# Own zeros, an identity without DMA, bias rows spread by GpSimd, and gate and value weights decoded as one block

## The chip, the cores and the metric

The kernel runs on one core of a Trainium2 chip. The metric is the device time of one execution in microseconds (us), the lower the better; the median of several runs is given. The engines are TensorE (PE, with its weight loads as PEld), VectorE (DVE), ScalarE (ACT), GpSimd (POOL) and SyncE (SP, which here only issues DMAs). Each engine takes its instructions strictly in the order in which they stand in its own program. DMAs are issued from the queues of SP, ACT and POOL and share 16 DMA engines.

## What is computed

Eight batches of eight heads, 576 positions, 64 dimensions a head, then a gated feed-forward layer over the 4608 tokens:

```python
scores = (1 / sqrt(D)) * q @ k.T                  # per batch and head, causal
cum = cumsum(maximum(s, 0.0), axis=-1)
bias = -(cum[:, :, :, None] - cum[:, :, None, :])
scores = where(causal, -1e9, scores + minimum(bias, 0.0))
attn = softmax(scores)                            # 1e-9 added to the sum
x = (attn @ v) with heads side by side            # 4608 x 512
gate = 1 / (1 + exp(-(x @ w_gate)))               # 512 x 1536
out = (gate * (x @ w_val)) @ w_out                # 1536 x 512
```

q, k, v and s are float32. The three weight matrices are float64, and the kernel reads them as pairs of 32-bit words.

## The kernel before

**The order of the work.** One loop of ticks (L673) runs through the 64 heads, five ticks a head, one for each tile of query rows (64, then four of 128). In a tick the code emits the scores of one tile, then for earlier tiles the mask, the row maximum, the exponential, and the product with v. Feed-forward units are placed between the ticks: a unit is one group of 256 tokens by one of 12 blocks of 128 hidden columns. The code runs through this program in its own order, and a scheduler then fixes the order of each engine's instructions and of the DMAs, before the run, by planned times; attention steps of the first heads carry a higher priority (`first()`), so weight work goes into gaps that the plan has. Nothing is reordered at run time.

**The start.** `ident` (L83 to L92) is the identity matrix with which PE transposes q, k, the exponentials and x. It is made by counting along a row (L88), writing the count to DRAM and reading it back as a column, `place` (L90, L91), and comparing the two (L92). `junk` (L95 to L97) is a buffer whose result nobody reads, and which takes one `affine_select` on POOL. The cumulative sums of the bias are made for all heads at once: s is loaded (L131), clipped (L133), and scanned against `zero` (L134 to L137); the result goes to a DRAM scratch, `cum_d` (L138). Tiles with one tag share its buffers: `junk`, `sp_sb`, `zero` and each head's `cr` have the tag "cr" with two buffers, so the third waits for the first.

**Bias rows.** For each head `load_crow` (L379) reads its row of `cum_d` and writes it to all 128 partitions with one DMA. `bias_row` (L416) subtracts the middle value of the row and multiplies, on DVE, into `rl`. `mask_part` (L424) then lets POOL write the causal limit into the columns of the tile on the diagonal, and the row maximum follows on DVE (L535 for the first eight heads, L437 for the others), which adds the bias row to the scores in PSUM.

**Two kinds of heads.** The first eight heads (`NN`) run in float32: q and k are transposed by PE (L509), scores are float32 matmuls (L526), the exponentials are transposed by PE (L546). The others use pairs of float16 parts and transposing DMAs (L371, L448, L480).

**Weights.** A step of `weight_step` loads one block of a matrix (128 partitions x 512 values, 512 KB as float64) from ACT's queue, turns float64 into float32 with one ACT and three DVE instructions (L233 to L236), sums squares on ACT (L242 or L263), adds them over the partitions on POOL (L246 or L265), forms a power-of-two scale with small DVE instructions (L117 to L127), and splits the block into float16 high (ACT, L256 or L270) and low part (DVE, L257 or L271). Gate and value blocks are separate steps; each has its own scale. The 24 steps of gate and value come first, then 12 of the output matrix. Six staging buffers serve the first 24 steps (two of their own and four in the space of the output weights), two the last 12. From tick `NE` = 44 the loop at L767 emits the units of the first two token groups, with the weight steps three blocks ahead; `hidden_scale` (L273) needs all value and output scales, and the output matmuls (L637) of those groups come after it.

## Time and profile before

| | |
|---|---|
| median of 3 runs | 1249.86 us (1247.86 to 1251.01) |
| the profiled execution | 1257.82 us, of which the span from first to last instruction is 1256.1 |
| granted TensorE clock, mean | 0.967 |
| busy share of the span: PE, DVE, ACT, POOL | 90%, 63%, 61%, 18% |
| DMA | 176.24 MB, mean 140 GB/s, 473412 packets |

The page cuts the span into 40 equal slices of 31.4 us; a digit is the busy share of a slice in tenths:

```profile
PE   1689778989998899989999999999999989999997
DVE  5998878775677757764665566766677667422221
ACT  4898866665666666764656466666676666332221
POOL 1343322221112121210111022212121211000000
PEclk9789889999999999999999999999999999999999
DMA  8764998995988789984665668878888966310000
```

PE is the busiest engine over the whole, but the slices differ: in the first ones DVE and ACT are as full as PE or fuller, and in the first slice PE has hardly begun. A group row of the profile reads: line, engine, operation, output<-input, shapes, how often | busy us in all, mean ns of one | idle time of the engine just before, and what ended most of it. A timeline row reads: start us, duration us, engine, line, operation; in brackets the idle time before it and what ended it.

### The profile page before, as it was taken

How to read it: one execution, taken by the hardware profiler on the slowest of the kernel's cores; microseconds unless marked ns; L12 is line 12 of the kernel's file. 1: busy time of each engine (PE TensorE's matmuls, PEld its weight loads, DVE VectorE, ACT ScalarE, POOL GpSimd, SP SyncE). 2: the span in 40 equal slices, each digit the busy share in tenths (PEclk: the TensorE clock that was granted, in tenths of full speed). 3: DMA queues.
4: the chain of work that ended last, by engine and by line, in shares of the span. 5: the costliest groups of instructions: out<-in, count | busy, mean ns of one | idle time of the engine just before them, and what ended most of it. 6: DMA issues, size and time to landing. Idle time of an engine off the chain costs nothing.

```text
span 1256.1 us, 30839 instructions
## 1 busy us (share of the span) xinstructions
PE 1127.7 (90%) x11924; PEld 875.9 (70%) x11924; DVE 789.6 (63%) x2291; ACT 761.5 (61%) x1553; POOL 227.3 (18%) x541
## 2 busy tenths in 40 slices
PE   1689778989998899989999999999999989999997
PEld 0467566666776787768777776767777777787775
DVE  5998878775677757764665566766677667422221
ACT  4898866665666666764656466666676666332221
POOL 1343322221112121210111022212121211000000
PEclk9789889999999999999999999999999999999999
DMA  8764998995988789984665668878888966310000
GB/s 255 238 179 142 181 188 156 182 181 128 162 164 166 160 161 171 177 163 101 115 146 110 129 143 166 164 154 174 160 163 172 170 118 134 56 29 2 18 18 17
DMA packets 473412, 176.24 MB, mean 140 GB/s; under 512 B 439601, under 2 KB 459058, under 8 KB 473266
## 3 DMA queue, kind: packets, MB, share of 16 engines
q1 hardware_dynamic: 453426, 136.53, 58.1%
q10 hardware_dynamic: 14400, 18.88, 4.9%
q0 software_dynamic: 5440, 18.88, 4.9%
q8 instruction: 93, 1.52, 0.5%
q14 instruction: 53, 0.43, 0.1%
HBM read 75.65 MB, written 9.59 MB: 68 GB/s over the span
## 4 chain that ended last, share of the span: by engine, by line
PE 28%; DMA 23%; issue 23%; ACT 11%; DVE 10%; POOL 2%; SPq 2%; POOLq 0%; ACTq 0%; DVEq 0%
PE gv L607 16%; DMA T<-qk 12%; PE o L637 7%; DMA qk<-in_q_dram 6%; DVE e L437 3%; ACT jq L339 2%; DMA T<-T 1%; DMA vsq<-in_v_dram 1%; PE s L412 1%; PE s L413 1%; ACT e L440 1%; ACT th L612 1%; DVE t L614 1%; ACT qk L366 1%; ACT vsq L151 1%
## 5 line engine op out<-in xcount | busy, mean ns | idle before, releaser
L607 PE MATMUL gv<-x,w 128*128 128x256 f16 (+3 forms) x6912 | 629.1, 249 | 17.1 <-DVE t L614 9.3
L607 PEld LDWEIGHTS <-w 128*128 128x128 f16 x6912 | 543.1, 99 | 78.1 <-issue 19.2
L637 PE MATMUL o<-w2all,h 128*128 128x512 f16 x1296 | 314.2, 379 | 3.2 <-ACT h L622 1.9
L427 POOL TENSOR_SCALAR_AFFINE_SELECT rl<-rl 128x128 f32<-128x128 f32 (+1 forms) x320 | 144.2, 451 | 496.2 <-DVE em L437 248.8
L637 PEld LDWEIGHTS <-h 128*128 128x128 f16 x1296 | 123.3, 98 | 110.9 <-ACT h L622 2.1
L440 ACT ACTIVATE e<-e,em 128x576 f32<-128x576 f32 x280 | 155.1, 556 | 72.6 <-DVE em L437 69.9
L614 DVE SCALAR_TENSOR_TENSOR t<-th,gv 128x256 f32<-128x256 f32 x192 | 80.1, 418 | 167.1 <-ACT th L612 166.7
L612 ACT ACTIVATE th<-gv,scb 128x256 f32<-128x256 f32 (+3 forms) x288 | 110.2, 408 | 117.2 <-PE gv L607 117.1
L437 DVE CUSTOM_DVE_ANT_0 e<-s,rl,qkcf 128x288 f32<-128x288 f32 x280 | 134.5, 484 | 25.4 <-PE s L412 9.7
L622 ACT ACTIVATE h<-t,hsc 128x256 f16<-128x256 f32 x192 | 96.9, 505 | 88.0 <-DVE t L614 87.8
L445 DVE SCALAR_TENSOR_TENSOR p<-e,p 128x1152 f16<-128x1152 f32 x112 | 129.9, 1159 | 31.9 <-ACT p L444 31.0
L623 DVE SCALAR_TENSOR_TENSOR h<-t,hsc,h 128x256 f16<-128x256 f32 x192 | 93.6, 488 | 42.2 <-ACT h L622 40.1
L412 PE MATMUL s<-T 128*128 128x288 f16 x336 | 88.3, 280 | 34.8 <-DVE em L437 29.6
L444 ACT ACTIVATE p<-e 128x1152 f16<-128x1152 f32 x112 | 111.8, 998 | 6.2 <-DMA pt<-p 4.0
L367 DVE SCALAR_TENSOR_TENSOR qk<-qk,qksc,qk 96x384 f16<-96x384 f32 x56 | 34.3, 613 | 104.5 <-ACT qk L366 104.4
L366 ACT ACTIVATE qk<-qk,qksc 96x384 f16<-96x384 f32 x56 | 34.4, 614 | 107.7 <-DMA T<-qk 107.5
L413 PE MATMUL s<-T 128*128 128x288 f16 x336 | 87.9, 283 | 10.8 <-DMA T<-T 10.8
L460 PE MATMUL av<-v,pt 128*128 128x65 f16 x840 | 85.7, 193 | 5.9 <-DMA pt<-p 5.8
L460 PEld LDWEIGHTS <-pt 128*128 128x128 f16 x840 | 77.5, 98 | 12.4 <-DMA pt<-p 7.0
L461 PE MATMUL av<-v,pt 128*128 128x64 f16 x840 | 85.6, 192 | 0.0
L462 PE MATMUL av<-v,pt 128*128 128x65 f16 x840 | 85.3, 194 | 0.0
L461 PEld LDWEIGHTS <-pt 128*128 128x128 f16 x840 | 77.4, 97 | 5.1
(187 smaller groups left out, 1215.3 us busy)
## 6 DMA issues: line engine op xcount, KB each, us to landing
cr<-cum_d SPq DMA_DIRECT2D x64, 288.0 KB, 4.3
vsq<-in_v_dram POOLq DMA_DIRECT2D x32, 288.0 KB, 4.3
out_dram<-osb POOLq DMA_DIRECT2D x36, 256.0 KB, 3.9
v<-in_v_dram SPq DMA_DIRECT2D x64, 128.0 KB, 3.7
qk<-in_q_dram SPq DMA_DIRECT2D x28, 288.0 KB, 3.8
qk<-in_k_dram SPq DMA_DIRECT2D x28, 288.0 KB, 4.8
T<-T SPq DMA_DIRECT2D x112, 72.0 KB, 2.6
ws<-in_moe_w_out_dram ACTq DMA_DIRECT2D x12, 512.0 KB, 4.0
```

The source lines that it names most:

```text
L412: nc.tensor.matmul(ps[:, : b_ - a], lhs, T[i][:, 0, a:b_], start=True, stop=False)
L413: nc.tensor.matmul(ps[:, : b_ - a], lhs, T[i][:, 2, a:b_], start=False, stop=True)
L427: nc.gpsimd.affine_select(rl[i][:, q0:w], rl[i][:, q0:w], pattern=[[-1, m]], compare_op=ALU.is_ge, fill=-MASKED if i < NN else MASKED, bas ...
L437: nc.vector.tensor_tensor_reduce(e_t[t][:, a:b_], ps[:, : b_ - a], rl[i][:, a:b_], c, init, ALU.add, ALU.min, acc)
L440: nc.scalar.activation(e_t[t][:, :w], e_t[t][:, :w], AF.Exp, bias=init, scale=-1.0)
L444: nc.scalar.activation(p_s[h_][:, 0], e_s[h_], AF.Copy, scale=PSCALE)
L445: nc.vector.scalar_tensor_tensor(p_s[h_][:, 1], e_s[h_], PSCALE, p_s[h_][:, 0], ALU.mult, ALU.subtract)
L460: nc.tensor.matmul(AV[i][:, t], hi, v_[:, D : 2 * D + 1], start=kb == 0, stop=False)
L461: nc.tensor.matmul(AV[i][:, t, 0:D], hi, v_[:, 0:D], start=False, stop=False)
L607: nc.tensor.matmul(ps[:, gv, a:e], w1[f][:, cc, gv, wl], x_of(b, cc)[:, xl, c0 + a : c0 + e], start=(c == 0), stop=(c == 3 * NC - 1))
L612: nc.scalar.activation(th[:, a:e], ps[:, 0, a:e], AF.Tanh, scale=scb[b][:, f : f + 1])
L637: nc.tensor.matmul(ps[:m], h[:, hl, tt * P : tt * P + m], w2[f][:, wl], start=(f == 0 and c == 0), stop=(f == NF - 1 and c == 2))
```

## The change

Six things are changed together.

1. `ident` is made on DVE alone: a count of 32 columns, transposed in blocks of 32 x 32 (`nc.vector.transpose`), and four comparisons of 32 x 32. `count` and `junk` lie in a buffer of the tag "x16"; the two DMAs and `place` are gone. The load of s is moved up to this place.
2. `zero` lies in a buffer of the tag "T", set before `sp_sb`.
3. The middle value is subtracted once for all heads (`rel`), and `rel` is what goes to DRAM.
4. `load_crow` reads one partition's row (for head 0 it takes the row in SBUF) and POOL spreads it with `partition_broadcast`. In the first eight heads that tile is the bias row; for the others `bias_row` only multiplies.
5. Gate and value block of one f are one step of 1024 columns, with one decode, one sum of squares, one scale and one split. There are 12 such steps and 12 of the output matrix; three staging buffers of twice the size serve the first 12, halves of one of them the last 12. `invw` and the new `wfield` have two rows in place of three, and the inverses of the scales are formed for three blocks at once (for the output matrix, twelve).
6. The pace of the steps changes: two at the first tick and six by tick 32; from tick 44 on, three at a time at every third f. As the list has 24 steps in place of 36, the bound `f + NF + WLA` (L775) now lets in all 12 output steps at unit 12; before it let in three there and one more at each unit after.

```diff
@@ -81,28 +81,30 @@
     for t, (q0, m, w) in enumerate(TILES):
         nc.gpsimd.memset(e_t[t][:, w:], 0.0)
     ident = cp.tile([P, P], F32, name="ident")
-    count = wp.tile([P, S], F32, tag="rl", name="count")[:, :P]
-    place = cp.tile([P, 1], F32, name="place")
-    nc.vector.memset(ident, 0.0)
-    nc.vector.memset(count, 1.0)
-    nc.vector.tensor_tensor_scan(count, count, ident, 0.0, ALU.add, ALU.add)
-    count_d = dp.tile([1, P], F32, name="count_d")
-    nc.sync.dma_start(count_d, count[0:1, :])
-    nc.sync.dma_start(place, count_d.rearrange("o n -> n o"))
-    nc.vector.tensor_scalar(ident, count, place, None, ALU.is_equal)
-    nc.gpsimd.memset(e_t[0][64:, :], 0.0)
-    junk = wp.tile([P, S], F32, tag="cr", name="junk")[:, :P]
+    scrap = wp.tile([P, 2, NTL * P], F16, tag="x16", name="scrap", bufs=1).bitcast(F32)
+    count, junk = scrap[:, 0, :P], scrap[:, 1, :P]
+    s_sb = wp.tile([NH, S], F32, tag="rl", name="s_sb")
+    nc.sync.dma_start(s_sb, s.rearrange("b h s -> (b h) s"))
     nc.gpsimd.memset(junk, 0.0)
     nc.gpsimd.affine_select(junk, junk, pattern=[[-1, P]], compare_op=ALU.is_ge, fill=0.0, base=0,
                             channel_multiplier=1)
+    nc.vector.memset(ident, 0.0)
+    nc.vector.memset(count[:, :64], 1.0)
+    nc.vector.tensor_tensor_scan(count[:, :32], count[:, :32], ident[:, :32], 0.0, ALU.add, ALU.add)
+    nc.vector.transpose(count[:, 32:64], count[:, :32])
+    for g in range(0, P, 32):
+        nc.vector.tensor_scalar(ident[g : g + 32, g : g + 32], count[g : g + 32, :32], count[g : g + 32, 32:33], None,
+                                ALU.is_equal)
+    nc.gpsimd.memset(e_t[0][64:, :], 0.0)
     expo = cp.tile([P, 2], F32, name="expo")
     nc.gpsimd.memset(expo[:, 0:1], 460.75)
     nc.gpsimd.memset(expo[:, 1:2], 204.75)
     ssq = [cp.tile([P, 2], F32, name=f"ssq{i}") for i in range(2)]
     for i in range(2):
         nc.gpsimd.memset(ssq[i], 0.0)
-    invw = cp.tile([P, 3, NF], F32, name="invw")
+    invw = cp.tile([P, 2, NF], F32, name="invw")
+    wfield = cp.tile([P, 2, NF], I32, name="wfield")
     hsc = cp.tile([P, NF], F32, name="hsc")
     gmax = cp.tile([P, 1], F32, name="gmax")
     cum_d = dp.tile([NH, S], F32, name="cum_d")
@@ -110,10 +112,11 @@
     def first(now=True):
         return tc.high_priority(1000) if now else ExitStack()
-    def field(ss, n, tag):
+    def field(ss, n, tag, f_=None):
         e = wp.tile([P, n], I32, tag=f"xe{n}", name=f"xe_{tag}")
-        f_ = wp.tile([P, n], I32, tag=f"xf{n}", name=f"xf_{tag}")
+        if f_ is None:
+            f_ = wp.tile([P, n], I32, tag=f"xf{n}", name=f"xf_{tag}")
         nc.vector.tensor_scalar(e, ss.bitcast(I32), 23, None, ALU.logical_shift_right)
         nc.vector.tensor_scalar(f_, e, -0.5, 204.75, ALU.mult, ALU.add)
         return f_
@@ -127,15 +130,17 @@
         nc.vector.tensor_scalar(dst.bitcast(I32), g_, 23, None, ALU.logical_shift_left)
-    s_sb = wp.tile([NH, S], F32, tag="rl", name="s_sb")
-    nc.sync.dma_start(s_sb, s.rearrange("b h s -> (b h) s"))
+    zero = wp.tile([P, 3, S], F16, tag="T", name="zero", bufs=2)[:NH, 0:2].rearrange("p a n -> p (a n)").bitcast(F32)
+    nc.vector.memset(zero, 0.0)
     sp_sb = wp.tile([NH, S], F32, tag="cr", name="sp_sb")
     nc.vector.tensor_scalar(sp_sb, s_sb, 0.0, None, ALU.max)
-    zero = wp.tile([NH, S], F32, tag="cr", name="zero")
-    nc.vector.memset(zero, 0.0)
     cum = wp.tile([NH, S], F32, tag="rl", name="cum")
     nc.vector.tensor_tensor_scan(cum, sp_sb, zero, 0.0, ALU.add, ALU.add)
-    nc.sync.dma_start(cum_d, cum)
+    rel = wp.tile([NH, S], F32, tag="rl", name="rel")
+    nc.vector.tensor_scalar(rel, cum, cum[:, S // 2 : S // 2 + 1], None, ALU.subtract)
+    nc.sync.dma_start(cum_d, rel)
     vch = H * S * D // P // S
@@ -184,97 +189,78 @@
     wst, wdec, wtot = {}, {}, {}
     t2first = [cp.tile([P, GT], F32, name=f"t2f_{u}") for u in range(2 * NF)]
...
+    raw0 = lp.tile([P, 8 * P, 2], I32, name="ws0")
+    dec0 = lp.tile([P, 8 * P], I32, name="wa0")
     flat = w2all.rearrange("p f l n -> p (f l n)").bitcast(I32)
...
+    raw = [raw0] + [flat[:, i * 16 * P : (i + 1) * 16 * P].rearrange("p (n t) -> p n t", t=2) for i in range(2)]
+    dec = [dec0] + [flat[:, i * 8 * P : (i + 1) * 8 * P] for i in range(4, 6)]
+    wsteps = [(0, f) for f in range(NF)] + [(1, f) for f in range(NF)]
+    def room(n):
+        o, f = wsteps[n]
+        if o == 0:
+            return raw[f % 3], dec[f % 3], n - 3
+        half = slice(f % 2 * 4 * P, (f % 2 + 1) * 4 * P)
+        return raw0[:, half], dec0[:, half], n - 2 if f > 1 else (NF - 1) // 3 * 3
     def load_weight(n):
...
+        o, f = wsteps[n]
         fs = slice(f * P, (f + 1) * P)
...
+        r, d, _ = room(n)
+        for x, src in enumerate((w_out,) if o else (w_gate, w_val)):
+            src = src[fs, :] if o else src[:, fs]
+            if wide:
+                src = src.bitcast(I32)
+                dst = r.rearrange("p n t -> p (n t)")
+            else:
+                dst = d.bitcast(F32)
+            if o == 0:
+                src = src.rearrange("(c p) n -> p c n", p=P)
+                dst = dst.rearrange("p (c x n) -> p c x n", c=NC, x=2)[:, :, x]
+            nc.scalar.dma_start(dst, src)
+    def decode_weight(n):
+        o, f = wsteps[n]
+        r, a, _ = room(n)
         if not wide:
...
+            return a.bitcast(F32)
+        m = w2[f].rearrange("p l n -> p (l n)") if o else w1[f].rearrange("p c g l n -> p (c g l n)")
+        m = m.bitcast(I32)
+        nc.scalar.activation(a.bitcast(F32), r[:, :, 1].bitcast(F32), AF.Copy, scale=2.0 ** -112)
+        nc.vector.tensor_scalar(m, a, 3, 0x7FFFFFF8, ALU.logical_shift_left, ALU.bitwise_and)
+        nc.vector.scalar_tensor_tensor(a, a, -0x80000000, m, ALU.bitwise_and, ALU.bitwise_or)
+        nc.vector.scalar_tensor_tensor(a, r[:, :, 0], 29, a, ALU.logical_shift_right, ALU.bitwise_or)
+        return a.bitcast(F32)
+    def split_weight(n, a):
+        o, f = wsteps[n]
+        if o:
+            hi, lo = w2[f][:, 0], w2[f][:, 1]
         else:
...
+            a = a.rearrange("p (c n) -> p c n", n=P)
+            hi, lo = (w1[f].rearrange("p c g l n -> p (c g) l n")[:, :, l] for l in range(2))
+        ss = wp.tile([P, 1], F32, tag="wss", name=f"wss{n}")
+        nc.scalar.activation(hi, a, AF.Square, accum_out=ss)
+        tot = wp.tile([P, 1], F32, tag="wst", name=f"wtot{n}")
+        nc.gpsimd.partition_all_reduce(tot, ss, P, ADD_REDUCE)
+        f_ = field(tot, 1, f"w{n}", wfield[:, o, f : f + 1])
+        sc = wp.tile([P, 1], F32, tag="wsc", name=f"wsc{n}")
         pow2(sc, f_)
...
+        nc.scalar.activation(hi, a, AF.Copy, scale=sc)
+        nc.vector.scalar_tensor_tensor(lo, a, sc, hi, ALU.mult, ALU.subtract)
+    def inverse_weights(o, fs):
+        inverse_pow2(invw[:, o, fs], wfield[:, o, fs], fs.stop - fs.start)
     def hidden_scale():
+        inverse_weights(1, slice(0, NF))
         g = wp.tile([P, NF], F32, tag="hsg", name="hsg")
...
+        nc.vector.tensor_tensor(g, invw[:, 0], invw[:, 1], ALU.mult)
         m = wp.tile([P, 1], F32, tag="hsm", name="hsm")
         nc.vector.tensor_reduce(m, g, mybir.AxisListType.X, ALU.max)
         nc.vector.tensor_scalar(gmax, m, 2.0 ** -100, None, ALU.max)
@@ -289,26 +275,14 @@
         osc[b] = wp.tile([P, 1], F32, tag="osc", name=f"osc{b}", bufs=3)
         nc.vector.tensor_scalar(osc[b], gmax, sv[b][1], 2.0 ** 15, ALU.mult, ALU.mult)
-    AHEAD = 3
     wnext = {"load": 0, "step": 0}
     def weight_step():
         n = wnext["step"]
-        kept = n - 1 if not wide and wsteps[n][1] == 1 else n
-        while wnext["load"] < min(n + AHEAD, len(wsteps)):
-            m = wnext["load"]
-            if m > n and any(slot_of(u, *stage) is slot_of(m, *stage) for u in range(kept, m)):
-                break
-            load_weight(m)
+        while wnext["load"] < len(wsteps) and room(wnext["load"])[2] < n:
+            load_weight(wnext["load"])
             wnext["load"] += 1
-        f, x = wsteps[n]
-        decode_weight(n)
-        if x < 2:
-            square_weight(f, x)
-            if x == 1:
-                split_weights(f)
-        else:
-            split_out_weight(f)
+        split_weight(n, decode_weight(n))
         wnext["step"] = n + 1
     def ffn_scale(b, fs=slice(0, NF)):
@@ -378,7 +352,9 @@
     def load_crow(i):
         crow[i] = wp.tile([P, S], F32, tag="cr", name=f"cr{i}")
-        nc.sync.dma_start(crow[i], cum_d[i : i + 1, :].to_broadcast([P, S]))
+        if i > 0:
+            nc.sync.dma_start(crow[i][0:1], cum_d[i : i + 1, :])
+        nc.gpsimd.partition_broadcast(crow[i], crow[i][0:1] if i > 0 else rel[0:1])
     def load_v(p):
         b, h0 = divmod(2 * p, H)
@@ -414,11 +390,11 @@
             S_ps[i, t].append((ps, a, b_))
     def bias_row(i):
+        if i < NN:
+            rl[i] = crow[i]
+            return
         r = wp.tile([P, S], F32, tag="rl", name=f"rl{i}")
-        nc.vector.tensor_scalar(r, crow[i], crow[i][:, S // 2 : S // 2 + 1],
-                                1.0 if i < NN else qkc[i // 2][1][:, 0:1], ALU.subtract, ALU.mult)
+        nc.vector.tensor_scalar(r, crow[i], qkc[i // 2][1][:, 0:1], None, ALU.mult)
         rl[i] = r
     def mask_part(i, t):
@@ -761,17 +737,18 @@
                     v_square(b + 1, h - 2)
                 if t == 4 and h == 6:
                     v_scale(b + 1)
-            while n < NE and wnext["step"] < min(int((n - 3) * 0.3), 9):
+            while n < NE and wnext["step"] < min(2 + n // 8, 6):
                 weight_step()
         if n >= NE and state["u"] < 2 * NF:
             fdone = min(NF, int((n - NE + 1) * FPT))
             while state["u"] < 2 * fdone:
                 f = state["u"]
-                if f < NF:
-                    while wnext["step"] < min(2 * (f + WLA), 2 * NF):
+                if f < NF and f % WLA == 0:
+                    while wnext["step"] < f + WLA:
                         weight_step()
-                    ffn_scale(0, slice(f, f + 1))
+                    inverse_weights(0, slice(f, f + WLA))
+                    ffn_scale(0, slice(f, f + WLA))
                 while f >= NF and wnext["step"] < min(f + NF + WLA, len(wsteps)):
                     weight_step()
                 emit_unit()
```

72 lines of the change are left out of this document (removed).

## The prediction

> **What bounds the kernel now.** I read the page's slices first (PE is nearly idle in the first of them), then a table of windows by stage, then the timeline of the first 45 us.
>
> ```profile
> 0.00:24.80 24.80, 0.04 (x1) 0.04 (x1) 11.08 (x27) 8.14 (x16) 6.01 (x26) 1.00 0.85 238
> 24.80:38.80 14.00, 6.42 (x18) 3.62 (x18) 13.41 (x34) 12.49 (x28) 1.99 (x3) 0.96 1.05 315
> 38.80:131.00 92.20, 77.49 (x440) 60.63 (x441) 83.48 (x300) 83.97 (x207) 33.31 (x72) 0.82 0.60 174
> 131.00:300.00 169.00, 142.21 (x1285) 105.11 (x1285) 124.25 (x390) 113.37 (x231) 40.60 (x91) 0.93 0.92 172
> 300.00:1000.00 700.00, 657.21 (x7598) 517.02 (x7596) 463.88 (x1311) 445.48 (x876) 128.61 (x314) 0.99 0.78 153
> ```
>
> A window row gives its length, the busy us of PE, weight load, DVE, ACT and POOL, then granted clock, DMA share and GB/s. PE idles for 24.8 us, then for 7.6 of 14; from 300 to 1000 it is 94% busy. So the long part belongs to PE, and the large hole is at the start. What holds PE there:
>
> ```profile
> 14.34 0.28 POOL L97 TENSOR_SCALAR_AFFINE_SELECT junk<-junk 128x128 f32<-128x128 f32 x1 [11.09 <-issue]
> 14.80 0.54 DVE L135 MEMSET zero<- 64x576 f32 x1 [7.04 <-POOL junk L97]
> 15.80 1.34 DVE L137 TENSOR_TENSOR_SCAN cum<-sp_sb,zero 64x576 f32<-64x576 f32 x1
> 22.17 0.83 SPq L381 DMA_DIRECT2D cr<-cum_d  x2
> 24.43 0.28 DVE L92 TENSOR_SCALAR ident<-count,place 128x128 f32<-128x128 f32 x1
> 24.76 1.22 PE L509 MATMUL nq_ps<-ident,nqk 96*128 96x96 f32 x6 [24.76 <-DVE ident L92]
> 30.47 3.75 PE L526 MATMUL s<-nk,nq 128*128 128x288 f32 x6 [1.69 <-ACT nk L516]
> 37.47 0.51 DVE L420 TENSOR_SCALAR rl<-cr 128x576 f32<-128x576 f32 x1
> 38.83 0.45 DVE L535 CUSTOM_DVE_ANT_0 e<-s,rl 128x288 f32<-128x288 f32 x1
> 39.34 1.43 PE L526 MATMUL s<-nk,nq 128*128 128x320 f32 x2 [5.12 <-DVE em L535]
> ```
>
> Two chains meet. The transposes wait for ident. The first scores are ready at about 34 and then wait for the bias row: zero waits for a buffer that junk holds, junk waits 11.09 us on POOL, then come the scan, a trip through DRAM, and a place behind weight decoding in DVE's order. The first row maximum starts at 38.83, and PE's next scores follow it at 39.34; that is the moment that moves.
>
> **The change part by part.**
>
> ```profile
> DMA to landing us min/median/max: 4.1/5.9/8.7
> 6.19 1.08 SPq L491 DMA_DIRECT2D nqk<-in_k_dram  x2
> 6.97 0.45 DVE L133 TENSOR_SCALAR sp_sb<-s_sb 64x576 f32<-64x576 f32 x1 [5.30 <-DMA s_sb<-in_s_dram]
> ```
>
> *Ident.* Two DMAs leave SP's queue; two memsets, a short scan, a transpose and four compares enter DVE. At 0.1 to 0.5 us each (the compare took 0.28; a DVE transpose has no row) they end before 4 us, while DVE waits for its first data anyway. Late next are q and k (the landing row is theirs): k issued at 6.19 lands by 10.3 to 14.9. From ident to the end of the first scores took 24.43 to 34.2, 9.8 us, so scores are ready at 20 to 25, the first of them some 3 us earlier.
>
> *Zero and the bias row.* With s landed at 6.97 and nothing to wait for, scan and rel follow: 0.45 + 1.34 + 0.51 (rel, by the L420 row) gives about 9.3. The DRAM trip is gone for row 0; the broadcast on POOL is in its place. So POOL is late next:
>
> ```profile
> L97 POOLq MODIFY_POOL_CONFIG  x2: 4/4/4, 3.3 to 3.3; - x2
> L246 POOLq MODIFY_POOL_CONFIG  x2: 23/23/23, 16.3 to 16.4; - x2
> 20.30 0.19 ACT L242 ACTIVATION_READ_ACCUMULATOR w<-w2all 128x1 f32 x1
> 22.20 0.91 POOL L246 PARTITION_ALL_REDUCE wtot<-wss  x1 [6.05 <-ACT w L242]
> L503 POOL MEMSET nq<- 64x576 f32 x8 | 4.5, 573 | 0.6 <-PE s L526 0.5
> L427 POOL TENSOR_SCALAR_AFFINE_SELECT rl<-rl x320: 240/297/1608, 39.1 to 1077.6; 128x128 f32<-128x128 f32 x128, 128x64 f32<-128x64 f32 x32
> ```
>
> POOL is reconfigured twice: at 3.3, with its next operation at 14.34 (11.0 us), and at 16.4, with its next at 22.20 though its input was ready at 20.49 (5.8 us). Afterwards masks and all-reduces alternate with no such row. A broadcast has no row; I take it to run under the second configuration, like the all-reduce (a rival below). Its own time lies between 0.24 and 1.6 us (ends of the L427 row); I take 0.7, near the 0.57 of the memset of as many columns. Then: junk's select ends at 14.6, +5.8, +0.7 gives 21.1, or 22.8 if 1.65 us of memsets stay ahead as before. The scores' end agrees. I put the first row maximum at 22.3: 16.5 us earlier than 38.83 (15 to 18).
>
> [...]
>
> *Does the gain pass through 38.8 to 131?* There DVE and ACT are 91% busy and PE 84%, so all three count.
>
> ```profile
> L234 DVE TENSOR_SCALAR w<-w2all 128x512 int32<-128x512 int32 x16 | 6.8, 423 | 1.3 <-ACT w2all L233 0.9 <-ACT w L242 0.4
> L236 DVE SCALAR_TENSOR_TENSOR w2all<-w2all 128x512 int32<-128x512 int32 x16 | 11.0, 686 | 0.1
> L257 DVE SCALAR_TENSOR_TENSOR w<-w2all,wsc,w 128x512 f16<-128x512 f32 x16 | 11.6, 743 | 0.4 <-ACT w L256 0.4
> L445 DVE SCALAR_TENSOR_TENSOR p<-e,p 128x1152 f16<-128x1152 f32 x56 | 76.1, 1359 | 24.9 <-ACT p L444 24.7
> L445 DVE SCALAR_TENSOR_TENSOR p<-e,p 128x768 f16<-128x768 f32 x56 | 53.8, 960 | 6.9 <-ACT p L444 6.3
> L256 ACT ACTIVATE w<-w2all,wsc 128x512 f16<-128x512 f32 x16 | 10.7, 718 | 0.0
> L444 ACT ACTIVATE p<-e 128x1152 f16<-128x1152 f32 x56 | 64.6, 1154 | 4.6 <-DMA pt<-p 4.0
> L444 ACT ACTIVATE p<-e 128x768 f16<-128x768 f32 x56 | 47.1, 842 | 1.6
> L420 DVE TENSOR_SCALAR rl<-cr 128x576 f32<-128x576 f32 x8 | 4.3, 536 | 2.0 <-ACT vsq L151 2.0
> ```
>
> The L445 pair gives DVE 1.04 ns a column, the L444 pair gives ACT 0.81. A gate and value pair costs DVE 2 x (0.42 + 0.69 + 0.69 + 0.74) = 5.1 us (L235 has L236's shape). At 1024 columns, 0.53 us more for each of three and about 0.28 more for the first, it is 0.70 + 1.22 + 1.22 + 1.27 = 4.4; twelve pairs save 8 us. On ACT three passes by the L256 row go from 2 x 0.72 to 1.13 each: 0.9 a pair, 11 in all. Eight bias rows (4.3 us) leave DVE too. In exchange less decoding is done by the first maximum: DVE was busy 24.5 us ahead of 38.8 and has about 12 us of work between 9.3 and 22.3. So the loads of this stage hardly change, and it stays 92 us long; I credit 2 us (none to 8). Gate and value of a block are now decoded together, so the first decode waits for two loads, not one; the bias chain covers that. The scales of three blocks are now inverted together, so the first tanh waits for the third block's scale. Cover for that is wide: the last gate and value split began at 102.6, the first gv matmul at 144.69.
>
> ```profile
> L257 DVE SCALAR_TENSOR_TENSOR w<-w2all,wsc,w x16: 734/744/752, 28.8 to 102.6; 128x512 f16<-128x512 f32 x16
> 144.69 1.15 PE L607 MATMUL gv<-x,w 128*128 128x256 f16 x9
> ```
>
> If that cover were gone, the last three decodes of 4.4 us on DVE would stand ahead of PE, 13 us.
>
> *Later heads.* The row that each head loads shrinks from 128 copies to one:
>
> ```profile
> cr<-cum_d SPq DMA_DIRECT2D x64, 288.0 KB, 4.3
> PE s L412 <- DVE em L437: 25.9, 29, 2.0
> DVE e L437 <- POOL rl L427: 3.0, 11, 1.0
> 203.07 0.71 DVE L271 SCALAR_TENSOR_TENSOR w2all<-wa,woc,w2all 128x512 f16<-128x512 f32 x1
> 211.92 0.38 PE L637 MATMUL o<-w2all,h 128*128 128x512 f16 x1
> ```
>
> 64 x 288 KB are 18.4 MB that no longer share the DMA engines with transposes; the share there is 0.78, so a fetch is seldom alone. I credit 1 us (none to 5), because PE is held by other things in that stage. POOL gains 56 late broadcasts. Each waits for its row's DMA with the masks queued behind it; em waits for the mask, PE for em. From 300 to 1000 masks held DVE for 3.0 us in all, and PE waited 25.9 us for em. I charge 2 us (none to 20).
>
> **Sum.** The profiled execution took 1257.8 us (span 1256.1 and 1.7 around it), 8 above the median of 1249.9. 1257.8 - 16.5 - 2 - 1 + 2 = 1240.3; the same 17.5 off the median gives 1232.4, forecast **1232**.
>
> **The rivals.**
>
> *A second wait at the hand-over (1240 to 1250, 0.17).* The first output matmul at 211.92 needs all output weights; their last split ran at 203.07, 8.1 us before. If decoding, which starts with less head start, ends only as early as now, the gain stops at those 8 us plus what the heads still absorb: 0 to 10. Against it: decoding gets 8 us lighter, and with 24 steps in place of 36 the bound at L775 asks for all output steps at unit 12, not over the ten units from there. It decides if the last split comes later than about 195.
>
> *A shorter first stage (1216 to 1226, 0.13).* If DVE and ACT truly bind the fp32 heads, the 12 and 11 us taken off them show, and the gain is 24 to 34. Against it: PE itself is 84% busy there.
>
> *POOL's queue becomes the wait (1254 to 1272, 0.11): slower.* A late row stops POOL, and five masks with it. It eats the 17.5 at 0.31 us a head over 56 heads; at 0.4 to 0.7 the time is 1254 to 1272. For it: landing of the old row took 4.3 us, and masks already stretch from 0.30 to 1.6. Against: a head lasts 16 us (64 heads from 39.1 to 1077.6), and its row is asked for a head ahead.
>
> [...]
>
> *The broadcast doesn't share the configuration (0.02).* Then each of 64 heads reloads twice, 64 x 2 x 5.8 = 742 us: about 1990.
>
> **How the numbers follow.** The forecast (1226 to 1240) has 0.56. Range 1218 to 1248: it holds it, most of the short stage and of the hand-over, so gains from 2 to 32 us. A measurement of this kernel tells some 0.3% (3.7 us) from no change: faster is 0.56 + 0.13 + 0.11 of the hand-over = 0.80; same is its other 0.06 and 0.01 left over; slower is 0.11 + 0.02.
>
> **What would show it.** Right: ident before 5 us, no wait of zero for junk, a second reconfiguration straight behind junk's select, the first row maximum at 21 to 24, the first gv matmul near 127 (was 144.7), no reconfiguration after. Wrong: POOL waiting for cr's DMA with masks behind, PE waits for em well over 26 us, the last output split after 195, or a broadcast over 1.6 us.

## The result and the profile after

The changed kernel takes 1221.02 us (median of 4 runs, 1216.57 to 1224.46); the kernel before, on the same chip, 1250.43. The ratio is 0.9733, with a 95% interval of 0.9691 to 0.9775: about 33 us faster, where 17.5 were forecast. The profiled run took 1222.6 us (span 1220.9), so that by span it is 35.2 us shorter than the profiled run before. Some 6 us of that lie in the executions that were profiled: the one before was 7.4 us above its median, the one after 1.6.

The table of windows, with the cuts of the prediction (length, busy us of PE, weight load, DVE, ACT, POOL, then clock, DMA share, GB/s):

```profile
0.00:24.80 24.80, 6.14 (x18) 3.71 (x18) 9.56 (x17) 7.91 (x12) 4.75 (x23) 1.00 0.90 253
24.80:38.80 14.00, 8.54 (x30) 6.69 (x31) 8.90 (x24) 8.87 (x17) 9.16 (x16) 1.00 0.63 191
38.80:131.00 92.20, 74.93 (x435) 61.56 (x433) 80.62 (x238) 83.68 (x178) 38.97 (x69) 0.81 0.58 163
131.00:300.00 169.00, 145.29 (x1509) 110.95 (x1510) 137.18 (x406) 122.75 (x250) 64.04 (x112) 0.98 0.81 163
300.00:1000.00 700.00, 666.54 (x7820) 525.04 (x7816) 475.72 (x1342) 455.54 (x894) 170.06 (x360) 1.00 0.72 139
```

Before 38.8 PE now has 14.7 us of work behind it instead of 6.5. From 38.8 to 131 it does a little less than before. From 300 to 1000 it runs 7820 matmuls where there were 7598: 2.9% more in the same 700 us, in a stage in which the forecast moved 1 us. (The kernel after is ahead when the window begins, so the window doesn't hold quite the same work; the cut by heads below does.) The timeline of the start:

```profile
2.10 0.99 DVE L97 TENSOR_SCALAR ident<-scrap 32x32 f32<-32x32 f32 x4
...
7.52 0.51 DVE L142 TENSOR_SCALAR rel<-cum 64x576 f32<-64x576 f32 x1
...
13.69 0.28 POOL L90 TENSOR_SCALAR_AFFINE_SELECT scrap<-scrap 128x128 f32<-128x128 f32 x1 [11.49 <-issue]
14.03 2.76 POOL L479 MEMSET nq<- 64x576 f32 x4
...
16.99 3.75 PE L502 MATMUL s<-nk,nq 128*128 128x288 f32 x6 [1.02 <-ACT nk L492]
...
24.93 0.86 POOL L357 PARTITION_BROADCAST cr<-rel  x1 [7.73 <-issue]
...
26.58 0.30 POOL L403 TENSOR_SCALAR_AFFINE_SELECT cr<-cr 128x128 f32<-128x128 f32 x1
26.87 0.35 POOL L248 PARTITION_ALL_REDUCE wtot<-wss  x1
...
27.25 0.15 DVE L120 TENSOR_SCALAR xe_w<-wtot 128x1 int32<-128x1 int32 x1 [10.84 <-POOL wtot L248]
27.36 1.23 DVE L234 SCALAR_TENSOR_TENSOR w2all<-w2all 128x1024 int32<-128x1024 int32 x1
...
28.56 0.45 DVE L511 CUSTOM_DVE_ANT_0 e<-s,cr 128x288 f32<-128x288 f32 x1
```

`ident` is done at 3.1, `rel` at 8.0, the first scores at 20.7. Everything then waits for POOL: it is reconfigured twice, and stands idle for 11.49 and 7.73 us before the operations behind that, with 3.2 us between, most of it memsets; the first row maximum starts at 28.56. DVE waits in the same hole: 10.84 us for an all-reduce that stands behind the broadcast. The hand-over (where feed-forward matmuls begin among the heads) and the late stage: first the first gv and output matmuls from the timeline, then the line of the low parts of the output weights, then PE's longest wait between 300 and 1000 (total, times, longest), which is for the row maxima `em`:

```profile
141.34 0.93 PE L583 MATMUL gv<-x,w 128*128 128x256 f16 x7
217.97 1.24 PE L613 MATMUL o<-w2all,h 128*128 128x512 f16 x5
```

```profile
L253 DVE SCALAR_TENSOR_TENSOR w2all<-wa,wsc,w2all x12: 737/745/799, 115.4 to 207.3; 128x512 f16<-128x512 f32 x12
```

```profile
PE s L388 <- DVE em L413: 18.0, 24, 1.3
```

To see where the time went I cut the run at the first row maximum of a head, the first, ninth, 25th and last of them (read from DVE's row-maximum rows, six a head). The rows of `rl` maxima show the ends of it, for before and after:

```profile
L437 DVE CUSTOM_DVE_ANT_0 e<-s,rl,qkcf x280: 269/511/686, 136.8 to 1080.4; 128x288 f32<-128x288 f32 x28, 128x320 f32<-128x320 f32 x28, 128x64 f32<-128x64 f32 x28, 128x448 f32<-128x448 f32 x28
```

```profile
L413 DVE CUSTOM_DVE_ANT_0 e<-s,rl,qkcf x280: 270/511/685, 134.5 to 1044.9; 128x288 f32<-128x288 f32 x28, 128x320 f32<-128x320 f32 x28, 128x64 f32<-128x64 f32 x28, 128x448 f32<-128x448 f32 x28
```

The first time is that of head 8, the last that of the last maximum of head 63. From the first maximum of head 63 on both kernels need the same 189.9 us. Before: 38.8 + 98.0 + 263.8 + 665.6; after: 28.6 + 105.9 + 246.1 + 650.4. So the start gained 10.2 us, the eight float32 heads gave 7.9 back, heads 8 to 24 (the hand-over to the feed-forward matmuls) gained 17.7, and heads 24 to 63 gained 15.2: 35.2 together. The windows of the third piece, heads 8 to 24, before and after:

```profile
136.80:400.60 263.80, 231.39 (x2449) 177.50 (x2447) 186.46 (x572) 174.59 (x353) 58.02 (x132) 0.95 0.90 169
134.50:380.60 246.10, 218.97 (x2432) 169.56 (x2432) 191.45 (x562) 175.06 (x354) 83.00 (x151) 0.99 0.80 160
```

PE is busy 12.4 us less there for nearly the same matmuls, at a granted clock of 0.99 in place of 0.95.

### The profile page after: what moved, and what is told of

It reads as the page before. It is cut to its first block, busy times and chain, and to the rows that moved or that the text cites. A ratio compares the mean times of both kernels' runs of the same rounds, so it can differ in the third digit from the quotient of the medians.

```text
span 1220.9 us, 30743 instructions
## 1 busy us (share of the span) xinstructions
PE 1114.0 (91%) x11924; PEld 871.3 (71%) x11924; DVE 783.0 (64%) x2194; ACT 756.7 (62%) x1505; POOL 299.4 (25%) x605
## 2 busy tenths in 40 slices
DMA packets 464177, 157.51 MB, mean 129 GB/s; under 512 B 438495, under 2 KB 457951, under 8 KB 464030
## 4 chain that ended last, share of the span: by engine, by line
PE 34%; issue 24%; DMA 18%; DVE 9%; ACT 8%; POOL 4%; SPq 1%; POOLq 0%; ACTq 0%; DVEq 0%
PE gv L583 17%; DMA T<-qk 10%; PE o L613 9%; DMA qk<-in_q_dram 3%; DVE e L413 3%; DMA cr<-cum_d 2%; PE s L388 1%; PE na_ps L531 1%; ACT jq L313 1%; PE s L389 1%; PE s L502 1%; DMA vsq<-in_v_dram 1%; POOL cr L357 1%; ACT qk L340 1%; POOL rl L403 1%
## 5 line engine op out<-in xcount | busy, mean ns | idle before, releaser
L583 PE MATMUL gv<-x,w 128*128 128x256 f16 (+3 forms) x6912 | 618.7, 247 | 13.6 <-DVE t L590 9.9
L583 PEld LDWEIGHTS <-w 128*128 128x128 f16 x6912 | 536.2, 98 | 70.5 <-issue 15.9
L403 POOL TENSOR_SCALAR_AFFINE_SELECT rl<-rl 128x64 f32<-128x64 f32 (+1 forms) x280 | 130.3, 466 | 380.1 <-DVE em L413 192.4
L598 ACT ACTIVATE h<-t,hsc 128x256 f16<-128x256 f32 x192 | 96.9, 505 | 92.0 <-DVE t L590 91.7
L421 DVE SCALAR_TENSOR_TENSOR p<-e,p 128x1152 f16<-128x1152 f32 x112 | 130.7, 1167 | 28.2 <-ACT p L420 27.6
L388 PE MATMUL s<-T 128*128 128x288 f16 x336 | 86.7, 277 | 29.2 <-DVE em L413 25.8
L389 PE MATMUL s<-T 128*128 128x288 f16 x336 | 86.0, 277 | 3.4 <-DMA T<-T 3.4
L436 PEld LDWEIGHTS <-pt 128*128 128x128 f16 x840 | 77.2, 98 | 13.1 <-DMA pt<-p 7.7
L357 POOL PARTITION_BROADCAST cr<-cr x63 | 63.7, 1014 | 80.5 <-DMA cr<-cum_d 79.7
```

Of the source, the lines that this page charges most:

```text
L388: nc.tensor.matmul(ps[:, : b_ - a], lhs, T[i][:, 0, a:b_], start=True, stop=False)
L389: nc.tensor.matmul(ps[:, : b_ - a], lhs, T[i][:, 2, a:b_], start=False, stop=True)
L403: nc.gpsimd.affine_select(rl[i][:, q0:w], rl[i][:, q0:w], pattern=[[-1, m]], compare_op=ALU.is_ge, fill=-MASKED if i < NN else MASKED, bas ...
L421: nc.vector.scalar_tensor_tensor(p_s[h_][:, 1], e_s[h_], PSCALE, p_s[h_][:, 0], ALU.mult, ALU.subtract)
L436: nc.tensor.matmul(AV[i][:, t], hi, v_[:, D : 2 * D + 1], start=kb == 0, stop=False)
L583: nc.tensor.matmul(ps[:, gv, a:e], w1[f][:, cc, gv, wl], x_of(b, cc)[:, xl, c0 + a : c0 + e], start=(c == 0), stop=(c == 3 * NC - 1))
```

## The experiments

Three theories stood at first: the start makes the gain and it only shows late; the rows make it, by the 18.7 MB that no longer cross the DMA engines (176.24 before, 157.51 after); the merged weight steps make it, by the load taken off DVE and ACT. All runs are beside runs of the kernel before on the same chip. The columns of stages are from the one profiled run of each, and the granted clock differs between these: in the stretch to head 8 it is 0.89 in a_oldstart, which takes 95.9 us, and 0.79 in a_oldstart_256, which takes 105.2. A difference of some us in one stage is therefore read only where several runs show it. "Address" is the remainder modulo 256 of the byte address at which the compiler placed the tile where queries and keys land (explained under the fourth group).

| run | median us | ratio [95%] | address | first max | to head 8 | 8 to 24 | 24 to 63 |
|---|---|---|---|---|---|---|---|
| before | 1250.43 | 1 | 0 | 38.8 | 98.0 | 263.8 | 665.6 |
| after | 1221.02 | 0.9733 [0.9691, 0.9775] | 0 | 28.6 | 105.9 | 246.1 | 650.4 |
| b_rows | 1242.41 | 0.9899 [0.9835, 0.9964] | 0 | 31.6 | 113.1 | 254.1 | 651.4 |
| a_dmarows | 1232.06 | 0.9827 [0.9768, 0.9885] | 0 | 29.0 | 105.5 | 247.7 | 661.0 |
| b_start | 1273.82 | 1.0150 [1.0077, 1.0223] | 224 | 35.3 | 108.4 | 262.1 | 677.2 |
| b_start_pad | 1252.37 | 1.0008 [0.9976, 1.0040] | 0 | 37.3 | 106.6 | 255.1 | 661.8 |
| b_weights | 1275.43 | 1.0174 [1.0109, 1.0238] | 32 | 36.9 | 102.4 | 268.6 | 678.4 |
| b_weights_pad | 1270.78 | 1.0150 [1.0100, 1.0200] | 64 | 37.1 | 102.5 | 263.0 | 672.7 |
| b_weights_pad96 | 1263.39 | 1.0090 [1.0058, 1.0122] | 128 | 37.4 | 96.9 | 265.1 | 667.3 |
| before_pad | 1273.93 | 1.0179 [1.0138, 1.0221] | 32 | 37.5 | 100.0 | 265.6 | 683.6 |
| a_oldweights | 1262.75 | 1.0087 [1.0049, 1.0126] | 224 | 29.7 | 104.7 | 259.8 | 676.1 |
| a_oldweights_pad | 1229.75 | 0.9818 [0.9783, 0.9853] | 0 | 30.2 | 104.8 | 254.7 | 647.9 |
| a_oldstart | 1243.14 | 0.9933 [0.9904, 0.9963] | 128 | 30.5 | 95.9 | 255.5 | 660.4 |
| a_oldstart_256 | 1237.90 | 0.9843 [0.9800, 0.9885] | 0 | 29.7 | 105.2 | 256.8 | 656.4 |
| a_qk32 | 1243.29 | 0.9891 [0.9832, 0.9950] | 32 | 28.9 | 105.0 | 251.3 | 669.8 |
| a_notqk | 1240.79 | 0.9881 [0.9839, 0.9923] | 128 | 29.4 | 105.7 | 252.2 | 666.5 |
| a_dummy | 1276.89 | 1.0196 [1.0136, 1.0255] | 0 | 29.2 | 151.8 | 249.7 | 657.9 |
| a_dummy16 | 1229.99 | 0.9835 [0.9788, 0.9882] | 0 | 28.2 | 109.5 | 249.0 | 650.3 |
| a_onelib | 1210.68 | 0.9678 [0.9625, 0.9731] | 0 | 18.4 | 102.0 | 245.3 | 654.0 |
| a_onelib_al | 1211.31 | 0.9655 [0.9618, 0.9692] | 0 | 17.3 | 102.1 | 248.4 | 651.0 |

**One part at a time.** Three kernels are the one before with one part of the change each: b_start (items 1 and 2), b_rows (items 3 and 4), b_weights (items 5 and 6). Two are the changed kernel with one part taken back. a_oldweights has the weight steps of before; a_dmarows copies the rows to all partitions by DMA again, from head 1 on:

```diff
-            nc.sync.dma_start(crow[i][0:1], cum_d[i : i + 1, :])
-        nc.gpsimd.partition_broadcast(crow[i], crow[i][0:1] if i > 0 else rel[0:1])
+            nc.sync.dma_start(crow[i], cum_d[i : i + 1, :].to_broadcast([P, S]))
+        else:
+            nc.gpsimd.partition_broadcast(crow[i], rel[0:1])
```

> The kernel before, with the bias rows alone changed: the middle value subtracted once, one row of 2.3 KB fetched for each head and spread by POOL. Traffic theory (most of the gain comes after 300 us, because 18.4 MB of row copies no longer share the DMA engines and SP's queue with transposes and loads): 1222 to 1236, with the lead over the kernel before growing steadily between 300 and 1050 us. Rival, order theory (the gain after 300 us is that of another order of instructions, from the new weight steps): within 6 us of 1250. Rival, start theory (the forecast's: the gain is at the first row maximum): 1240 to 1250, since zero still waits for junk.

> The kernel before, with the start alone changed: identity on DVE without DMA, zero in a buffer of its own, s loaded first. Start theory: the first row maximum moves from 38.8 to about 22 to 30 (the DRAM trip of the first row stays) and 1236 to 1244 results. Traffic and order theory: the first row maximum moves as much, but little arrives at the end: 1244 to 1252.

> The kernel before, with the weights alone changed: gate and value of a block as one step of 1024 columns, new staging and pace. Traffic theory: nothing after 300 us, 1244 to 1254. Order theory: 1225 to 1240. Start theory: 1244 to 1252.

> The changed kernel with the weights loaded, decoded and split as before (24 + 12 steps). If the weights' part helps beside the others: 1226 to 1240. If it costs as it does alone (plus 21 us): 1200 to 1210. If nothing: within 5 us of 1221.

> The changed kernel, but from head 1 on the row is again written to all 128 partitions by one DMA of 288 KB, without POOL. Traffic theory: the lead after 300 us is lost, 1236 to 1246. Order theory: within 6 us of 1221. Start theory: within 6 us of 1221.

The rows agree from both sides: alone they take 1.0% off, and with the copies back the ratio rises by 0.0094 (the two intervals just touch). Both fall short of what the traffic theory expected (1222 to 1236, and 1236 to 1246), so the rows are a part of the gain and not most of it. It is the late stage: 651.4 against 665.6, and 661.0 against 650.4. The window from 300 to 1000 in a_dmarows, and PE's longest wait there:

```profile
300.00:1000.00 700.00, 657.61 (x7624) 516.23 (x7622) 463.95 (x1318) 448.60 (x880) 127.40 (x314) 0.99 0.78 155
```

```profile
PE s L389 <- DVE em L414: 27.9, 31, 2.6
```

The DMA share is 0.78 again (0.72 after), and PE waits 27.9 us for row maxima instead of 18.0. It isn't another order of the work: from head 24 on PE's instructions stand in the same order in both kernels, and those of DVE and ACT differ at one place each. Start and weights, however, each made the kernel slower alone, by 1.5 and 1.7%, and without the weight part the changed kernel lost 42 us. No theory had that, and most of the loss was in heads 24 to 63, long after every step that those parts touch.

**More bytes, by themselves.** The changed kernel with one more copy a head into a DRAM tile of its own, of the old size (a_dummy) or of 64 bytes for each of 128 rows (a_dummy16):

```diff
+            spare = dp.tile([P, S], F32, name=f"sp{i}")
+            nc.sync.dma_start(spare, cum_d[i : i + 1, :].to_broadcast([P, S]))
```

> The changed kernel, and beside each one-row load the old copy of 288 KB too, written to a scratch in DRAM that nobody reads, from the same queue. Heads 24 to 63 took 650 us from first row maximum to first row maximum in the changed kernel and 661 with the copies as the only source. Traffic theory (the bytes and their packets on the DMA engines cost the late heads time): heads 24 to 63 take 660 or more, 1231 to 1240. POOL theory (what helps is that DVE and the masks are served better by the broadcast on POOL, the DMA is hidden): 1217 to 1225.

> The same extra DMA for each head with 128 rows of 64 bytes in place of 2304: as many rows to issue, 8 KB in place of 288. Traffic theory by bytes: as the changed kernel, 1217 to 1225. Issue theory (128 rows cost SP's queue or the DMA engines as much when small): as the run with full copies, 1231 to 1240. Order theory (any edit moves the plan of later heads by 10 us or more): either kernel off by 8 us or more in either direction, without a step between them by bytes.

Neither tells what was asked. The copies have no buffer to wait for, so all 63 were issued by 116.4 and 98.7 us; the list of issues of a_dummy between 40 and 120 has

```profile
sp<-cum_d SPq DMA_DIRECT2D x52, 288.0 KB
```

and its window near the end of them

```profile
80.00:100.00 20.00, 6.25 (x25) 4.73 (x26) 9.46 (x23) 5.74 (x13) 2.95 (x3) 0.51 1.04 315
```

With the DMA engines full (their share is 1.04) PE is busy 6.25 of 20 us: the early heads take 46 us longer. About the late stage these two say nothing, as no copy was left by then; the 657.9 and 650.3 there can't tell bytes from any other cost of the copies. Why a_dummy16 is 0.0102 above the changed kernel by the ratios wasn't followed up; its order of work differs from the early heads on.

**One configuration.** The changed kernel with an all-reduce in place of junk's select, so that the first operation for which POOL is configured (its first MODIFY_POOL_CONFIG stands at 2.2 us in both kernels) already is of the kind that it needs later:

```diff
-    nc.gpsimd.affine_select(junk, junk, pattern=[[-1, P]], compare_op=ALU.is_ge, fill=0.0, base=0,
-                            channel_multiplier=1)
+    nc.gpsimd.partition_all_reduce(junk[:, 1:2], junk[:, 0:1], P, ADD_REDUCE)
```

> The changed kernel with junk's affine_select replaced by a partition all-reduce of one column, whose result nobody reads either, so that POOL may be configured once only. Reconfiguration theory (the first row maximum at 28.6 is late by a second reconfiguration of 7.7 us): one pair of reconfiguration rows, first row maximum at 18 to 21, and if start gains pass on, 1210 to 1215. Rival (start gains are taken back by 140 us, as PE's lead of 14 us at 100 fell to 3 at 140 in the changed kernel): within 5 us of 1221.

The timeline of its start:

```profile
2.28 0.39 POOL L90 PARTITION_ALL_REDUCE scrap<-scrap  x1
...
10.02 0.86 POOL L356 PARTITION_BROADCAST cr<-rel  x1
...
18.43 0.46 DVE L510 CUSTOM_DVE_ANT_0 e<-s,cr 128x288 f32<-128x288 f32 x1 [0.56 <-PE s L501]
```

Both gaps are gone, not one: neither the all-reduce nor the broadcast nor the first mask behind it waits on "issue". The first row maximum is at 18.4, as soon as the scores of its tile are there, and the kernel takes 1210.68 us: 40 less than before and, by medians, 10 less than the changed one (0.55% by the ratios, whose intervals overlap; for a_onelib_al below, with the same start, 0.78%). PE, DVE and ACT have the same order of instructions in it as in the changed kernel, so that the gain is the start's. Between the select of junk and the broadcast the changed kernel had a second wait, of 7.73 us; between the all-reduce and the broadcast there is none. With the pools behind moved by 32 bytes as well, to multiples of 128 (a_onelib_al), nothing more is gained, 0.9655 against 0.9678:

> a_onelib (the changed kernel with one GpSimd configuration instead of two) with 32 bytes more at the end of the second pool, so that the pools behind it (th, h, the output rows, four of ten x tiles), 96 past a multiple of 128 so far, begin at a multiple of 128 too. If every tile that a transfer fills or reads counts: 1195 to 1206. If only landings of queries, keys, values and rows count, which were aligned before: as a_onelib, 1207 to 1214.

**The address.** In b_start and before, the engines' instructions of the late stage stand in the same order, and yet the one is 12 us slower there. What differs is where the compiler put the tiles. Tiles are taken from pools, which lie one behind the other in the memory on the chip. Dropping `place` shortens the first pool by 32 bytes a partition; `invw` and `wfield` lengthen it by 32. One alone moves every tile of the second pool; in the changed kernel they cancel. A pad tests it:

```diff
+    pad = cp.tile([P, 8], F32, name="pad")
+    nc.gpsimd.memset(pad, 0.0)
```

> The kernel before with one unused tile of 32 bytes a partition more in the first pool (cp), zeroed once by GpSimd, so that the tiles of the second pool (wp: T, qk, cr, xq, pt) begin 32 bytes past a multiple of 64 instead of at one; no other instruction changes. Address theory: the stretch from the first row maximum of head 24 to that of head 63, 666 us in the kernel before, becomes about 677, as in b_start, b_weights and a_oldweights, which all have these tiles there; the landing of queries and keys (before: 3.75 and 4.02 us) goes to 4.3 to 5.7, and the wait of ScalarE for qk from 21 to about 35 us; time 1260 to 1275, ratio 1.01 to 1.02. Rival (the edits themselves, or the hour of the run): 666 us and a ratio within 0.997 to 1.003.

> b_start (before with zeros of their own, the identity by transposes and the score bias loaded first) with the same 32 bytes, which here bring the tiles back to multiples of 64. Address theory: head 24 to head 63 falls from 677 to about 661 to 666 us and the time from 1274 to 1250 to 1262, ratio about 1.00 to 1.006. Rival (the start itself costs the later heads time): still 677 us and a ratio of about 1.015.

> b_weights (before with only the merged decoding of the weights) with the same 32 bytes, tiles again at multiples of 64. Address theory: head 24 to head 63 falls from 678 to 661 to 666 us, time from 1275 to 1250 to 1264, ratio 1.00 to 1.01. Rival (the merged weight steps slow what comes after): still 678 us, ratio about 1.017.

> a_oldweights (the changed kernel with the weight steps of before) with the same 32 bytes, tiles again at multiples of 64. Address theory: head 24 to head 63 falls from 676 to about 650 us, time from 1263 to 1232 to 1240, ratio 0.985 to 0.99; what is left above the 1221 of the changed kernel is then the price of the weight steps. Rival (the merged weight steps are worth the 42 us that separate the two): still 676 us and a ratio of about 1.009.

The pad alone makes the kernel before 1.8% slower, takes the whole 1.5% from b_start, and 33 us from a_oldweights. In each of these pairs the four engines run the same instructions in the same order, but for the memset of the pad, so that nothing but the address is left. Only b_weights_pad hardly moved; its tiles came to lie 64 past a multiple of 128. ScalarE's waits for queries and keys between 300 and 1000 (`jq` is its first reading of what has landed), in before, before_pad, b_start and b_start_pad:

```profile
ACT jq L339 <- DMA qk<-in_q_dram: 20.8, 19, 1.9
ACT jq L339 <- DMA qk<-in_k_dram: 1.0, 1, 1.0
```

```profile
ACT jq L341 <- DMA qk<-in_q_dram: 33.5, 19, 3.6
ACT jq L341 <- DMA qk<-in_k_dram: 5.8, 16, 0.7
```

```profile
ACT jq L338 <- DMA qk<-in_q_dram: 34.4, 20, 3.6
```

```profile
ACT jq L340 <- DMA qk<-in_q_dram: 20.6, 20, 1.9
```

And the list of issues (size, median us to landing) in before, then in before_pad:

```profile
qk<-in_q_dram SPq DMA_DIRECT2D x20, 288.0 KB, 3.7
qk<-in_k_dram SPq DMA_DIRECT2D x20, 288.0 KB, 4.0
```

```profile
qk<-in_q_dram SPq DMA_DIRECT2D x20, 288.0 KB, 4.5
qk<-in_k_dram SPq DMA_DIRECT2D x20, 288.0 KB, 5.5
```

The same transfer takes up to 38% longer (5.5 us against 4.0 for the keys) when its tile starts 32 bytes off. Each head row of q and k lands as pieces of 64 float32, 256 bytes (of the 473412 packets of before 439601 are under 512 bytes). By remainder the keys land in 4.0 us at 0, 5.5 at 32 and at 64 (b_weights_pad), 5.1 at 224 (b_start), and 4.7 at 128 (b_weights_pad96, discussed next):

```profile
qk<-in_k_dram SPq DMA_DIRECT2D x20, 288.0 KB, 4.7
```

So by these medians the keys landed 0.7 to 1.5 us later at all four other remainders that were tried; why is not shown.

**Which tile, which multiple.** b_weights_pad96 and a_oldstart (the changed kernel with the start of before) have 96 bytes of pad, at 128 past a multiple of 256; a_oldstart_256 has 224, at a multiple of 256. In a_qk32 pads of 32 bytes ahead of the tile `qk` and 96 behind it move that tile by 32, in a_notqk pads of 32 at the front and 96 and 32 around `qk` move the others (the edit of a_qk32; the pads are also zeroed once):

```diff
+            pada = wp.tile([P, 8], F32, tag="pada", name="pada", bufs=1)
...
         t = wp.tile([QP, 2, QC, 2, D], F32, tag="qk32", name=f"nqk_{p}", bufs=1)
...
+            padb = wp.tile([P, 24], F32, tag="padb", name="padb", bufs=1)
```

> b_weights (before with only the merged weight steps) with 96 bytes more in the first pool, so that the landing tiles of queries, keys, values and rows begin at a multiple of 128, as in before and in the changed kernel; in b_weights they are 32 past a multiple of 64, in b_weights_pad 64 past a multiple of 128. If the address must be a multiple of 128: head 24 to head 63 falls from 678 and 673 to about 662 us, time 1238 to 1256, ratio 0.99 to 1.005. Rival (the merged steps cost the later heads 15 us by themselves): still 672 to 678 us and 1265 to 1276.

> The changed kernel with 32 bytes ahead of the tile in which queries and keys land and 96 behind it, so that this tile alone is 32 past a multiple of 128 and all others stay at the same remainder as in the changed kernel. If it is the landing of queries and keys that suffers: head 24 to head 63 goes from 650 to about 670 us and the time from 1221 to 1235 to 1250. Rival (another tile's address, or the landing of values): 650 us and 1218 to 1225.

> The complement: every tile of that pool 32 past a multiple of 64, and only the one in which queries and keys land back at a multiple of 128. If the landing of queries and keys is what suffers: 650 to 655 us from head 24 to head 63 and 1219 to 1230. Rival: 665 to 677 us and 1240 to 1265.

> The changed kernel with the start of before (identity by a counted row and a DMA, zeros in the rows' buffer, score bias behind it) and 96 bytes more in the first pool, so that the landing tiles lie at multiples of 128 as in the changed kernel. If the earlier start comes through: first row maximum at 31 to 38 instead of 28.6, time later by as much as 3 to 10 us, 1224 to 1232, ratio 0.977 to 0.984. If it is lost in the fp32 heads, as it was in b_start_pad: 1218 to 1223, ratio 0.972 to 0.976.

> a_oldstart with the landing tiles at a multiple of 256 bytes, where they are in before and in the changed kernel; a_oldstart has them 128 past one. If 256 is what counts: head 24 to head 63 falls from 660 to 648 to 652 us and the time from 1243 to 1221 to 1232, and what is left above 1221 is the price of the old start. Rival (128 is enough, and the old start costs 22 us by way of the order of work behind it): 660 us and 1238 to 1246, as a_oldstart.

Neither 1.0090 for b_weights_pad96 nor its 667.3 us fits the one expectation or the other: from 64 to 128 the ratio falls from 1.0150, with intervals that overlap, and doesn't reach 1. By the ratios moving `qk` costs 1.6% (20 us), nearly as much as moving everything, with PE, DVE and ACT in the order of the changed kernel. But moving the others costs 1.5%. Neither is a clean test: in a_notqk `qk` lies at 128, in a_qk32 the tiles behind it are moved by 128, and whether 128 hurts is what the last pair was for. That `qk` alone is enough is likely and not shown. From a_oldstart to a_oldstart_256 ScalarE's wait for queries falls as in the pads above,

```profile
ACT jq L314 <- DMA qk<-in_q_dram: 29.3, 21, 2.9
ACT jq L314 <- DMA qk<-in_k_dram: 3.1, 10, 0.6
```

```profile
ACT jq L314 <- DMA qk<-in_q_dram: 19.9, 19, 2.7
```

and the ratio by 0.9%, with intervals that don't overlap; yet the late stage moves by only 4 us, and the runs of both scatter by 12 us and more (the profiled run of a_oldstart is the fastest of its twelve). Nor is this pair clean: the longer pad gave the scheduler another plan, and 994 of the 11924 places in PE's order hold another kind of matmul, all ahead of head 24. So at 128 the wait for queries was longer (29.3 us against 19.9) and, in b_weights_pad96, the landing of the keys too (4.7 us against 4.0 in before); what that costs in time isn't isolated. The ratios' intervals give 0.4 to 1.4% for address and order together, and the expectation of 648 to 652 in the late stage failed. Both expectations for a_oldstart failed too: 1243.14 is above either.

What the pairs at a good address say of the parts: without the rows 0.9827, without the weight part 0.9818, without the new start 0.9843, with all three 0.9733. By these ratios each is worth 11 to 14 us where the other two are there. Alone the rows are worth as much, the start nothing (1.0008), and the weight part no gain (1.0090, at 128). Why the start and the weight part pay only together is open; the next section has what the traces say.

## Why the prediction was right and wrong

By stages the sum had -16.5 to the first row maximum, -2 in the float32 heads, nothing at the hand-over and +1 in the late heads. The profiled pair had -10.2, +7.9, -17.7 and -15.2. That the time, 1221.02, lies inside the range of 1218 to 1248 is luck: the first two terms promised too much, the last two far too little, and these errors cancel in part.

**The direction and the start's chain: right.** ident, zero, rel and the second reconfiguration went as described, and POOL was what came late.

**The first row maximum: 16.5 forecast, 10.2 measured.** The term was mis-sized. The forecast 22.3 was 14.6 for the end of the select, 1.2 for memsets, 5.8 and 0.7. Measured: 13.97, 3.23 (not 1.2) between the select and the second wait, 7.73 (not 5.8), 0.86 (not 0.7), which is 25.79; then 2.8 us that weren't in the sum. In those the mask and an all-reduce follow on POOL, and DVE has that all-reduce's result and a piece of decoding ahead of the maximum. a_onelib shows that neither of the two waits was needed. And the 10.2 are hardly the work of ident and zero, to which the prediction gave them: in a_oldstart_256, with the old ident (done at 24.1) and the old zero, the first row maximum comes at 29.7, and in b_start, with the new ones alone, at 35.3. The first gv matmul, expected near 127, came at 141.34; in a_onelib it comes at 127.72.

**"The loads of this stage hardly change, and it stays 92 us long; I credit 2": wrong in its second half.** The loads came out as forecast (DVE 80.6 for 83.5, ACT 83.7 for 84.0 in the same window), but from the first maximum to head 8 it took 105.9 us, not 98.0. DVE did 18.5 us of work by 38.8 where it had done 24.5: it stood 10.84 us behind POOL's second configuration. The prediction saw that less decoding is done early and called it paid for. In a_onelib, without that hole, the stage takes 102.0, so the hole explains about half of the 7.9 us. The rival of a shorter first stage gave about the measured time, by a mechanism that the trace denies.

**"I credit 1 us (none to 5) ... I charge 2 us": the step that failed.** The rows were to cost 1 us and gained 11 to 13 (a_dmarows and b_rows), the largest error that an experiment isolates. I argued that PE is held by other things. It is held by row maxima, 25.9 us in that stage, and the copies lengthen that wait: in a_dmarows, where they alone come back, it is 27.9 us instead of 18.0, and heads 24 to 63 take 10.6 us more with PE's order unchanged. By what path the copies do it, full DMA engines or another, isn't shown, since a_dummy and a_dummy16 didn't reach that stage. The row that should have been weighed was the DMA share of 0.78 in the long stage, of which each head's 288 KB were a part: it is 0.72 without them (their bytes were 18.7 MB by the two pages, not 18.4).

**POOL's queue as the wait: denied.** POOL did wait for the row's transfer with the masks behind it:

```profile
L357 POOL PARTITION_BROADCAST cr<-cr x63: 855/857/2189, 36.4 to 992.2; - x63
...
its engine sat idle before it (us, times) until:
  DMA cr<-cum_d: 79.7, 47
```

79.7 us in 47 waits, 1.3 us for each of 63 rows, and PE's wait for maxima fell: a row is asked for a head ahead, and the masks have that much room. "POOL waiting for cr's DMA" was named as a sign of failure and isn't one; nor is "a broadcast over 1.6 us", as the longest took 2.19 and the median 0.86. The sign that counts was em.

**The hand-over: the sum had no term for it, and it moved most.** Of the second wait, a rival, the condition came and the price didn't. The last split started at 207.3 (past 195) and the first output matmul at 217.97, 6 us later than before. Still heads 8 to 24 gained 17.7. In all kernels at address 0 that lack start or weights or both that stretch takes 254 to 264 us; in those with both 245 to 250. So about half of the 17.7 comes back from kernel to kernel. Two things go with it, and no run separates them. The scheduler gave another order there: between the first maxima of heads 17 and 18 stand 72 output matmuls before, 97 without the new start, 103 without the new weight steps, and 23 in the changed kernel, with 68 behind them. And PE itself is faster: in the first group it is busy 227 to 231 us there at a granted clock of 0.937 to 0.962, in the second 219 to 226 at 0.955 to 0.986. (Over whole executions the clock is alike in the kernels before and after, 0.96 to 0.98.) Whether the order brings the clock, and what either is worth, wasn't tried; the cause of this step stays open.

## What to carry to other kernels

A transfer that runs beside a busy engine can cost time though nobody waits for it for long: the copies of the rows were worth 11 to 13 us here, so price such a transfer also by what it may hold up, and try it alone. Before trying parts of a change one by one, compare the addresses of the tiles in which transfers land: a tile of 32 bytes that comes or goes moved this kernel by 1.8%, more than any part of the change. And try an operation of the kind that is used later as the first one for which GpSimd is configured: here an all-reduce in place of a select brought the first row maximum from 28.6 to 18.4 us.
